# Planning a fixed issue order by a rehearsal with measured spacings: an attention and SwiGLU kernel on one core

## The chip, the cores and the metric

The kernel runs on one core of a Trainium2 chip. The metric is the device time of one execution in microseconds (us), as the median of several runs. The core has five engines that matter here, each with its own stream of instructions: TensorE (PE in the profile; its weight loads have a row of their own, PEld), VectorE (DVE), ScalarE (ACT), GpSimd (POOL) and SyncE (SP), which issues most transfers. [...]The program fixes the order of instructions on each engine.

## The reference

An attention over 32 inducing points is followed by a feed-forward block:

```python
# x (4, 12416, 128), inducing (32, 128)
def mab(q, kv):                       # softmax attention, scale 1/sqrt(C)
    s = scale * (q @ kv.transpose(0, 2, 1))
    a = np.exp(s - s.max(-1, keepdims=True))
    a /= a.sum(-1, keepdims=True) + 1e-09
    return a @ kv
h = mab(inducing, x)                  # 32 rows per batch
y = mab(x, h)                         # 12416 rows per batch
# then, with 49664 rows y, d_model 128, d_ff 1536:
yn   = y / sqrt(mean(y * y) + 1e-6) * rms_g
g    = yn @ w_gate                    # 128 -> 1536
val  = yn @ w_val                     # 128 -> 1536
out  = (g * sigmoid(g) * val) @ w_out # 1536 -> 128
```

## The kernel before

The rows of y are never made. Since y is a weighted sum of the 32 rows of h, the kernel multiplies h into the gate and value weights once a batch (`sg`, `sv`). What flows through the feed-forward block is the weights of the second attention, `a`.

**Units and slots.** Each of 4 batches has 25 units of up to 512 rows. d_ff is cut into 12 blocks of 128. One unit and one block make a *slot*: a gate matmul, a silu, a value matmul, a multiplication, and later a product with the block of `w_out`, which adds up over the 12 blocks in the PSUM tile `acc`. There are 1200 slots: 960 of 512 columns, 192 of 480 and 48 of 256.

```python
def slot(j, products, steps, tanh):
    g = bank()                                            # one of 5 PSUM banks
    nc.tensor.matmul(g[:, 0:T], sg[:, ts(j, P)], a[:, 0:T], start=True, stop=True)      # L681
    sl = silp.tile([P, 512], F32, name="silu")
    ...                                                   # (a variant with tanh, cut)
        nc.scalar.activation(sl[:, 0:T], g[:, 0:T], AF.Silu)                            # L689
    products()                                            # up to two products of earlier slots
    v = bank()
    nc.tensor.matmul(v[:, 0:T], sv[:, ts(j, P)], a[:, 0:T], start=True, stop=True)      # L692
    t = v if kinds.get((b, u, j)) == "sums" else up.tile([P, 512], F32, name="u")
    ...
        nc.vector.tensor_tensor(out=t[:, 0:T], in0=sl[:, 0:T], in1=v[:, 0:T], op=ALU.mult)   # L698
    steps()                                               # attention work, later parts of earlier slots
    if (b, u, j) in ready:
        soon(1, lambda: three(j, t))
    else:
        plain.append(lambda: project(wo[:, j, :], t[:, 0:T]))
```

**Kinds of blocks.** The product with `w_out` needs full fp32. A *plain* block does it as one fp32 product, which the trace shows as L616 x2. A *split* block takes the multiplied values apart into `hi`, `lo` and their difference `d`, and does three one-pass products in their place (L636, L638 and L616 with `more`). The first two add up in the single PSUM bank `u3` (shown as `u` on L636 and L638), the third in `acc`. The parts are made in two ways: "sums" on ScalarE, VectorE and one POOL operation, with the values left in their PSUM bank; "differences" with two operations on ScalarE and two on POOL.

```python
def three(j, t):
    while kws.get("out", 0) == RING:                      # RING = 4 places for hi, lo, d
        kara.pop(0)[1]()
    ...
    if kind == "sums":
        nc.scalar.activation(hi, v, AF.Copy, scale=(1.0 - 2.0 ** -13) * 2.0 ** -12)     # L663
        nc.vector.scalar_tensor_tensor(out=lo, in0=hi.bitcast(F32), scalar=-4096.0, in1=v, ...)   # L664
    else:
        up_ = third.tile([P, 512], F32R, name="hs")[:, 0:T]         # pool of one buffer
        nc.scalar.activation(up_, v, AF.Copy, scale=1.0 - 2.0 ** -13)                   # L668
        nc.gpsimd.tensor_tensor(out=lo, in0=v, in1=up_.bitcast(F32), op=ALU.subtract)   # L669
    def rest():
        if kind != "sums":
            nc.scalar.activation(hi, up_.bitcast(F32), AF.Copy, scale=2.0 ** -12)       # L673
        nc.gpsimd.tensor_tensor(out=d, in0=hi.bitcast(F32), in1=lo.bitcast(F32), op=ALU.subtract)  # L674
        kara.append((ready[b, u, j], lambda: project3(j, hi, lo, d)))
    soon(1, rest)
```

`soon(1, ...)` puts a step one slot later. When a unit's last split product is in, L641 (ScalarE) copies `u3` out.

**Which blocks are split, and when products are issued.** This is settled when the program is made. `loads` holds an estimate of each engine's work in each slot; a block is split, by sums if that fits and by differences if not, where the backlog of the next eight slots stays within LIMIT. `ready` is an estimated slot from which the product may be issued. In each slot `products()` then takes one or two of the waiting products, between the gate and the value matmul:

```python
loads = [[1.3, .68, .6, 0.0] ...]                         # us a slot: TensorE, VectorE, ScalarE, POOL
LIMIT = (0, 1.2, 1.2, 3.8)
RING, RESERVE = 4, 3
def products():
    now = b * NU * NJ + k
    count = max(len(plain) - 1, 0) + sum(at <= now for at, _ in kara)
    ...                                                   # exceptions near the exponentials, cut
    spare = ... else RESERVE
    for _ in range(min(count, 2 if count > spare else 1)):
        if kara and kara[0][0] <= now:
            kara.pop(0)[1]()
        else:
            plain.pop(0)()
```

**The seam.** Once for each of the attention sets (28 in all), the steps turn_a, square, turn_z, scale, apply, turn_b and split prepare the `a` of the next units. `scale` ends with the reciprocal root on POOL (L519, `rs`), which waits for a VectorE result of the same step (`ms`, L517). `apply` uses it on POOL too (L523). Before the change both stand in one slot.

**The next batch** runs its first attention and its weights beside the slots of the batch before; the fourth batch has none beside it.

Of the kernel before, what the change touches and what calls it, by code (L numbers as in the profile page):

```python
# [18 lines left out]
P = 128  # L19
R = 4  # L20
# [4 lines left out]
def kernel(  # L25
# [75 lines left out]
    RING, RESERVE = 4, 3  # L101
# [14 lines left out]
    third = pool("third", 1)  # L116
    silp = pool("silp", 3)
    up = pool("up", LAG + 3)
# [370 lines left out]
    def seam(b, s):  # L489
# [24 lines left out]
        def scale():  # L514
            ms = numbers("ms")
            nc.vector.reduce_sum(out=ms, in_=st["z"][rows, :, :], axis=AX.X)
            nc.vector.tensor_scalar(out=ms, in0=ms, scalar1=1.0 / C, scalar2=1e-6, op0=ALU.mult, op1=ALU.max)  # L517
            rs = st["rs"] = numbers("rs")
            nc.gpsimd.tensor_tensor(out=rs, in0=ms, in1=mhalf[rows, 0:n], op=ALU.pow)  # L519
# [18 lines left out]
        return [turn_a, square, turn_z, scale, apply, turn_b, split]  # L538
# [26 lines left out]
    def soon(k, step):  # L565

        waiting.append([k, step])
# [35 lines left out]
    def ffn(b, u):  # L603
# [6 lines left out]
        nk = sum((b, u, j) in ready for j in range(NJ))  # L610
# [43 lines left out]
        def three(j, t):  # L654

            while kws.get("out", 0) == RING:
                kara.pop(0)[1]()
            kws["out"] = kws.get("out", 0) + 1
            n = kws["n"] = (kws.get("n", 0) + 1) % RING
            hi, lo, d = (kws[name][:, n, 0:T] for name in ("hi", "lo", "d"))  # L660
            v, kind = t[:, 0:T], kinds[b, u, j]
            if kind == "sums":
                nc.scalar.activation(hi, v, AF.Copy, scale=(1.0 - 2.0 ** -13) * 2.0 ** -12)  # L663
                nc.vector.scalar_tensor_tensor(out=lo, in0=hi.bitcast(F32), scalar=-4096.0, in1=v,  # L664
                                               op0=ALU.mult, op1=ALU.add)
            else:
                up_ = third.tile([P, 512], F32R, name="hs")[:, 0:T]
                nc.scalar.activation(up_, v, AF.Copy, scale=1.0 - 2.0 ** -13)  # L668
                nc.gpsimd.tensor_tensor(out=lo, in0=v, in1=up_.bitcast(F32), op=ALU.subtract)  # L669

            def rest():
                if kind != "sums":
                    nc.scalar.activation(hi, up_.bitcast(F32), AF.Copy, scale=2.0 ** -12)  # L673
                nc.gpsimd.tensor_tensor(out=d, in0=hi.bitcast(F32), in1=lo.bitcast(F32), op=ALU.subtract)  # L674
                kara.append((ready[b, u, j], lambda: project3(j, hi, lo, d)))

            soon(1, rest)

        def slot(j, products, steps, tanh):
            g = bank()  # L680
# [9 lines left out]
            products()  # L690
# [9 lines left out]
            if (b, u, j) in ready:  # L700
                soon(1, lambda: three(j, t))
            else:
                plain.append(lambda: project(wo[:, j, :], t[:, 0:T]))
# [76 lines left out]
    turn_a, square, turn_z, scale, apply, turn_b, split = seam(0, 0)  # L780
# [6 lines left out]
    scale()  # L787
    weight[0, 1]["sign"]()
# [13 lines left out]
    if B > 1:  # L802
        for _ in range(R):
            load_channels(*pieces[1].pop(0))

    COST = {"turn_x": (0, .65), "scores1": (1.1, .7), "max2": (0, .85), "exp1_of": (0, 0, 1.3), "turn_e": (0, .69),
            "sum_h": (1.5, .29), "divide": (0, .8), "turn_h": (0, .8), "square_h": (0, .75), "stack": (1.1, 1.38),
            "scores2": (1.1, .69), "row_max": (0, .65), "sub_max": (0, 0, 0, 1.05), "exp2": (0, 0, 1.1), "table": (0, 0, 1.3),
            "turn_a": (0, .68), "square": (.9,), "turn_z": (0, 1.35), "scale": (0, .85, 0, 2.8), "apply": (0, 0, 0, 1.05),
            "turn_b": (0, .68), "split": (0, 0, .6, 1.26), "power": (0, .6), "power_number": (0, 0, .75), "upper": (0, .6),  # L810
            "upper_number": (0, 0, .65), "sign": (0, .7), "lower": (0, .7, 0, 1.3), "stack_of": (.9, 0, .6),
            "stack_low": (0, .7), "split_wo": (0, 0, .8, 1.6), "finish": ((0, .7, .6), (0, .7)),
            "sums": ((-.16,), (0, .7, .62), (0, 0, 0, 1.27)), "differences": ((-.16,), (0, 0, .63, 1.27), (0, 0, .63, 1.27))}
    loads = [[1.3, .68, .6, 0.0] for k in range(B * NU * NJ + 16)]

    def load(k, name, sign=1):
        cost = COST.get(name, ())
        for i, one in enumerate(cost if cost and isinstance(cost[0], tuple) else (cost,)):
            for e, us in enumerate(one):
                loads[k + i][e] += sign * us  # L820

    def schedule(b):
# [4 lines left out]
        def add(k, step, *args):  # L827
            plan.setdefault(int(k), []).append(lambda: step(*args))
            load(b * NU * NJ + int(k), step.__name__)

        def exponentials(k, step, first):
# [6 lines left out]
            for at in (k, k + len(groups)):  # L838
                load(b * NU * NJ + at, "table")
# [53 lines left out]
    for k, (b, s) in enumerate(order):  # L893
# [5 lines left out]
        for late_by, one in enumerate(following):  # L899
            for i, step in enumerate(seam(*one)):  # L900
                j = ((14, 17, 18, 21, 21, 29, 31) if k else (32, 33, 34, 35, 35, 39, 41))[i]
                n, j = divmod(j, NJ)
                at = (b, firsts[s] + n + late_by, j)
                seams.setdefault(at, []).append(step)
                load((b * NU + at[1]) * NJ + j, step.__name__)
# [7 lines left out]
    LIMIT = (0, 1.2, 1.2, 3.8)  # L913
    kinds, ready = {}, {}
    behind, out_at = [0.0] * 4, []

    def fits(k, kind):

        def ahead():
            now = list(behind)  # L920
            for i in range(k, k + 8):
                now = [max(0.0, x + one - loads[i][0]) for x, one in zip(now, loads[i])]
                yield list(now)

        before = list(ahead())
        load(k, kind)
        if all(x <= max(most, y + 0.1) for now, old in zip(ahead(), before) for x, y, most in zip(now, old, LIMIT)):
            return True
        load(k, kind, -1)

    for b, u in flat:
        load((b * NU + u + 1) * NJ + 4, "finish")
    for b, u in flat:
        marks = plans[b][1]
        for j in range(NJ):
            n = u * NJ + j
            k = b * NU * NJ + n
            out_at = [at for at in out_at if at >= k]
            if not (j >= NK or b == 0 and (u < 2 or n < 26) or (b, u) == flat[-1] and j > 6 or len(out_at) >= RING or
                    any(n - 1 <= e <= n + 3 for e in marks)):  # L940
                for kind in ("sums", "differences"):
                    if fits(k, kind):
                        kinds[b, u, j] = kind
                        left, last, at = behind[3], k + 2, k
                        for at in range(k, last):
                            left = max(0.0, left + loads[at][3] - loads[at][0])
                        late = 1.4 + left + loads[last][3] + max(behind[1:3])
                        at = last
                        while late > 0.1:
                            late -= loads[at][0]  # L950
                            at += 1
                        ready[b, u, j] = at
                        out_at.append(ready[b, u, j] - 1)
                        break
            for e in range(1, 4):
                behind[e] = max(0.0, behind[e] + loads[k][e] - loads[k][0])

    for b in range(B):
        plan, marks = plans[b]

        order = [(u, j) for u in range(NU) for j in range(NJ)]
        if not b:
            order[:2 * NJ] = sorted(order[:2 * NJ], key=lambda one: (one[1] // R, one))
        unit = {}
        for k, (u, j) in enumerate(order):

            def steps():
# [7 lines left out]
                for step in plan.get(k, ()):  # L975
                    step()
                for step in seams.get((b, u, j), ()):
                    step()
# [3 lines left out]
            def products():  # L982


                now = b * NU * NJ + k
                count = max(len(plain) - 1, 0) + sum(at <= now for at, _ in kara)
                hold = any(k < e <= k + 2 for e in marks)
                if hold and count < LAG:
                    return
                spare = 1 if any(e <= k < e + 4 for e in marks) or (b, u) == flat[-1] else RESERVE  # L990
                for _ in range(min(count, 2 if count > spare else 1)):
                    if kara and kara[0][0] <= now:
                        kara.pop(0)[1]()
                    else:
                        plain.pop(0)()
# [4 lines left out]
    while kara or plain:  # L1000
        (plain.pop(0) if plain else kara.pop(0)[1])()
# [32 lines left out]
```

## Time and profile before

| | before |
|---|---|
| time, median of 3 runs | 1706.56 us (1705.57 to 1708.16) |
| span of the profiled run | 1706.2 us |
| mean granted TensorE clock | 0.995 |
| VectorE, ScalarE, POOL busy | 80%, 71%, 69% |
| split blocks | 612 of 1200: 415 by sums, 197 by differences |
| `hs` of ScalarE (L668), idle before | 88.8 us, of which 68.5 waiting for POOL L669 |
| root on POOL (L519), 28 times | 2709 ns mean, 134.5 us idle before |

How to read it: "busy" is the time in which an engine has at least one instruction running. A line such as `PE acc L616 <- POOL xn L674` names who waited, writing what, and for whose instruction; behind the colon are the total in us, how often, and the longest. Names such as `xn` can stand for other things than the code's: the ring of hi, lo and d lies in the buffers `xn`. A timeline line has the start, the duration, the engine, the line and operation, and in brackets the idle time before it with its releaser. A count x2 means that two instructions in a row were merged. Ends of matmuls are modelled and overlap the next start.

### The profile page before, as it was taken

Reading aid. Unit: us, or ns where it says so; the run is one execution under the profiler, and the core shown is the slowest. Engines: PE = TensorE matmul, PEld = TensorE weight load, DVE = VectorE, ACT = ScalarE, POOL = GpSimd, SP = SyncE. Lnnn points to the kernel's source line nnn. Section 1 sums busy time; section 2 is a strip of 40 time slices with the busy share of each in tenths; the row PEclk is TensorE's granted clock in tenths of the full one; section 3 lists DMA queues with packets and bytes.
Section 4 is the critical chain, followed back from the end, with each engine's and each line's share of the span. In section 5 each row is a group of like instructions: output and inputs, shape, how many; then the busy total and the mean of one; then the engine's idle time right before and its main releaser. Section 6 shows DMA issues by size and latency. Waiting matters only on the chain. (4 is left out here: it accounts for less than half of the span.)

```text
span 1706.2 us, 24769 instructions
## 1 busy us (share of the span) xinstructions
PE 1649.8 (97%) x6992; PEld 1063.0 (62%) x6992; DVE 1371.8 (80%) x2350; ACT 1214.5 (71%) x2247; POOL 1173.4 (69%) x944
## 2 busy tenths in 40 slices
PE   8989999999999999999999999999999999999998
PEld 6546666656575665665667666556566666666666
DVE  5878887788788887778878888778878888888887
ACT  4557777667686676666768676667677787787776
POOL 1347784768486674577758675477757888888886
PEclk9999999999999999999999999999999999999999
DMA  6345524343443141524335324153211212112211
GB/s 249 87 68 82 103 46 97 73 97 58 70 77 67 31 88 29 128 66 81 67 53 82 55 40 84 31 122 84 54 30 30 38 32 38 34 29 38 37 32 28
DMA packets 389177, 112.47 MB, mean 66 GB/s; under 512 B 365073, under 2 KB 369713, under 8 KB 386481
## 3 DMA queue, kind: packets, MB, share of 16 engines
q1 hardware_dynamic: 388304, 110.82, 32.9%
q8 instruction: 55, 0.90, 0.2%
q14 instruction: 82, 0.66, 0.1%
q10 hardware_dynamic: 736, 0.08, 0.0%
HBM read 53.95 MB, written 27.00 MB: 47 GB/s over the span
## 5 line engine op out<-in xcount | busy, mean ns | idle before, releaser
L674 POOL TENSOR_TENSOR xn<-xn,xn 128x512 fp32r<-128x512 f32 (+2 forms) x612 | 758.1, 1253 | 247.1 <-DVE xn L664 133.5
L689 ACT ACTIVATE silu<-gv 128x512 f32<-128x512 f32 (+2 forms) x1186 | 687.4, 584 | 309.1 <-PE gv L681 296.0
L692 PE MATMUL gv<-a,sv 128*128 128x512 f32 (+2 forms) x1188 | 676.7, 570 | 4.8 <-ACT silu L689 3.8
L698 DVE TENSOR_TENSOR u<-silu,gv 128x512 f32<-128x512 f32 (+2 forms) x771 | 510.0, 665 | 190.1 <-PE gv L692 126.3
L616 PE MATMUL acc<-u,wo 128*128 128x512 f32 (+1 forms) x1176 | 587.7, 584 | 4.5 <-DVE u L698 4.3
L681 PE MATMUL gv<-a,sg 128*128 128x512 f32 (+2 forms) x1188 | 487.1, 410 | 4.3 <-ACT silu L689 2.6
L681 PEld LDWEIGHTS gv<-a,sg 128*128 128x128 f32 x1188 | 224.4, 189 | 209.4 <-ACT silu L689 54.5
L698 DVE TENSOR_TENSOR gv<-silu,gv 128x512 f32<-128x512 f32 (+2 forms) x415 | 277.7, 672 | 94.0 <-PE gv L692 61.6
L692 PEld LDWEIGHTS gv<-a,sv 128*128 128x128 f32 x1188 | 225.0, 189 | 169.4 <-issue 81.0
L664 DVE SCALAR_TENSOR_TENSOR xn<-xn,gv 128x512 fp32r<-128x512 f32 (+2 forms) x415 | 273.0, 658 | 7.3 <-ACT xn L663 3.9
L663 ACT ACTIVATE xn<-gv 128x512 fp32r<-128x512 f32 (+2 forms) x415 | 242.5, 584 | 47.0 <-DVE gv L698 40.9
L669 POOL TENSOR_TENSOR xn<-u,hs 128x512 fp32r<-128x512 f32 (+2 forms) x197 | 249.2, 1265 | 28.5 <-ACT hs L668 18.1
L616 PE MATMUL acc<-xn,more 128*128 128x512 f32 (+2 forms) x612 | 245.7, 401 | 23.0 <-POOL xn L674 22.8
L616 PEld LDWEIGHTS acc<-u,wo 128*128 128x128 f32 x1176 | 220.2, 189 | 60.4 <-issue 8.8
L636 PE MATMUL u<-xn,xn 128*128 128x512 f32 (+2 forms) x612 | 237.9, 389 | 4.2 <-ACT o L641 3.8
L668 ACT ACTIVATE hs<-u 128x512 fp32r<-128x512 f32 (+2 forms) x197 | 122.7, 623 | 88.8 <-POOL xn L669 68.5
L519 POOL TENSOR_TENSOR rs<-ms,mhalf 128x16 f32<-128x16 f32 (+2 forms) x28 | 75.9, 2709 | 134.5 <-DVE ms L517 122.8
L616 PEld LDWEIGHTS acc<-xn,more 128*128 128x128 f32 x612 | 115.1, 188 | 71.6 <-POOL xn L674 50.7
L636 PEld LDWEIGHTS u<-xn,xn 128*128 128x128 f32 x612 | 115.2, 188 | 33.3 <-ACT o L641 10.2
L638 PE MATMUL u<-xn,xn 128*128 128x512 f32 (+2 forms) x321 | 124.3, 387 | 0.0
L673 ACT ACTIVATE xn<-hs 128x512 fp32r<-128x512 f32 (+2 forms) x197 | 121.2, 615 | 0.0
L638 PE MATMUL u<-xn,more 128*128 128x512 f32 (+2 forms) x291 | 113.2, 389 | 0.0
(150 smaller groups left out, 1062.3 us busy)
## 6 DMA issues: line engine op xcount, KB each, us to landing
out_dram<-o SPq DMA_DIRECT2D x320, 64.0 KB, 2.0
xT<-in_x_dram SPq DMA_DIRECT2D x60, 256.0 KB, 4.7
xn<-in_x_dram SPq DMA_DIRECT2D x60, 256.0 KB, 4.9
a<-hi SPq DMA_DIRECT2D x156, 64.0 KB, 2.0
a<-lo SPq DMA_DIRECT2D x156, 64.0 KB, 2.0
xn<-in_x_dram SPq DMA_DIRECT2D x5, 1024.0 KB, 10.0
xn<-w SPq DMA_DIRECT2D x18, 256.0 KB, 3.0
out_dram<-o SPq DMA_DIRECT2D x64, 60.0 KB, 2.0
```

The lines of the kernel that those rows point to most:

```text
L616: nc.tensor.matmul(acc[:, 0:T], lhsT, rhs, start=st["left"] == NJ, stop=st["left"] == 1)
L636: nc.tensor.matmul(ups[:, 0:T], weight_of(0, j), hi, start=st["k"] == nk, stop=False)
L638: nc.tensor.matmul(ups[:, 0:T], weight_of(1, j), lo, start=False, stop=not st["k"])
L663: nc.scalar.activation(hi, v, AF.Copy, scale=(1.0 - 2.0 ** -13) * 2.0 ** -12)
L664: nc.vector.scalar_tensor_tensor(out=lo, in0=hi.bitcast(F32), scalar=-4096.0, in1=v, op0=ALU.mult, op1=ALU.add)
L668: nc.scalar.activation(up_, v, AF.Copy, scale=1.0 - 2.0 ** -13)
L669: nc.gpsimd.tensor_tensor(out=lo, in0=v, in1=up_.bitcast(F32), op=ALU.subtract)
L674: nc.gpsimd.tensor_tensor(out=d, in0=hi.bitcast(F32), in1=lo.bitcast(F32), op=ALU.subtract)
L681: nc.tensor.matmul(g[:, 0:T], sg[:, ts(j, P)], a[:, 0:T], start=True, stop=True)
L689: nc.scalar.activation(sl[:, 0:T], g[:, 0:T], AF.Silu)
L692: nc.tensor.matmul(v[:, 0:T], sv[:, ts(j, P)], a[:, 0:T], start=True, stop=True)
L698: nc.vector.tensor_tensor(out=t[:, 0:T], in0=sl[:, 0:T], in1=v[:, 0:T], op=ALU.mult)
```

## The change

All costs are replaced by spacings read from traces, and the planning by a rehearsal: while the program is made, a small model walks through all slots with a clock for each engine, decides the kind of each block by the backlog it sees, and notes for each slot which products go ahead of the gate matmul and which ahead of the value matmul. The program then follows these notes. Besides, the number of blocks held outstanding goes from three to six, with one more `u` buffer; the root becomes a step of its own; and the single buffer `hs` goes, its place taken by the block's own `d`.

```diff
-    RING, RESERVE = 4, 3
+    RING, RESERVE = 4, 6
-    third = pool("third", 1)
-    up = pool("up", LAG + 3)
+    up = pool("up", LAG + 4)
...
+            st["ms"] = ms
+
+        def root():
             rs = st["rs"] = numbers("rs")
-            nc.gpsimd.tensor_tensor(out=rs, in0=ms, in1=mhalf[rows, 0:n], op=ALU.pow)
+            nc.gpsimd.tensor_tensor(out=rs, in0=st["ms"], in1=mhalf[rows, 0:n], op=ALU.pow)
...
-            while kws.get("out", 0) == RING:
-                kara.pop(0)[1]()
+            assert kws.get("out", 0) < RING
...
-                up_ = third.tile([P, 512], F32R, name="hs")[:, 0:T]
-                nc.scalar.activation(up_, v, AF.Copy, scale=1.0 - 2.0 ** -13)
-                nc.gpsimd.tensor_tensor(out=lo, in0=v, in1=up_.bitcast(F32), op=ALU.subtract)
+                nc.scalar.activation(d, v, AF.Copy, scale=1.0 - 2.0 ** -13)
+                nc.gpsimd.tensor_tensor(out=lo, in0=v, in1=d.bitcast(F32), op=ALU.subtract)
...
         def slot(j, products, steps, tanh):
+            products(0)
             g = bank()
...
-            products()
+            products(1)
             v = bank()
...
-    loads = [[1.3, .68, .6, 0.0] for k in range(B * NU * NJ + 16)]
+    TAIL = {"PE": .17, "DVE": .09, "ACT": .11, "POOL": .04}
+    MADE = {"sums": ((-.16,), (0, .6, .49), (0, 0, 0, 1.25)), "differences": ((-.16,), (0, 0, .53, 1.25), (0, 0, .52, 1.25))}
+    loads = [[1.29, .6, .5, 0.0] for k in range(B * NU * NJ + 24)]
...
-                j = ((14, 17, 18, 21, 21, 29, 31) if k else ...)[i]       # slots of the seam's steps
+                j = ((14, 17, 18, 21, 22, 23, 29, 31) if k else ...)[i]
...
-    LIMIT = (0, 1.2, 1.2, 3.8)
+    LIMIT = (0, 0.8, 0.8, 2.6)
+    def rehearse():
+        ...
+        def issue(kind, to):
+            ...
+            if kind == "plain":
+                end = run("PE", 0.858 * w, t)
+            else:
+                if st["three"] == 0:
+                    run("PE", 0, split["u3"])
+                end = run("PE", 0.697 * w, t)
+        ...
+        def choose(to, most):              # up to `most` products that are ready, split ones first
+        def fill(to, until):               # products ahead of a bank that comes free later than 0.25 us from now
+            while until > at["PE"] + 0.25:
+                now = at["PE"] + 0.05
+                kind = next((kind for kind in ("three", "plain") if has(kind, now)), None)
+                if kind is None:
+                    break
+                issue(kind, to)
+        ...
+        def slot(b, k, u, j, tanh):
+            kind = decide(b, k, u, j)      # by the backlog of the modelled clocks and LIMIT
+            first, second = picks[b, k] = [], []
+            gi = bank()
+            fill(first, free[gi])
+            g = run("PE", 0.2325 * w, free[gi])
+            silu = run("ACT", 0.5 * w, g)
+            ...
+            least = 1 if near(...) or (b, u) == flat[-1] else RESERVE + 2 * near(b, k, -2, 0)
+            choose(second, min(2, max(0, split["all"] - least + 1)))
+            ...
+            fill(second, free[vi])
+            v = run("PE", 0.2325 * w, free[vi])
+            t = run("DVE", 0.6 * w, v, silu)
...
-            def products():
-                ...                        # the rule by counts, shown above
+            def products(some):
+                for kind in picks[b, k][some]:
+                    (plain if kind == "plain" else kara).pop(0)()
```

## The prediction

> **What bounds the kernel now.** I read the busy shares first, then TensorE's timeline, then the waits, then the groups.
>
> ```profile
> PE 1649.8 (97%) x6992; PEld 1063.0 (62%) x6992; DVE 1371.8 (80%) x2350; ACT 1214.5 (71%) x2247; POOL 1173.4 (69%) x944
> ```
>
> TensorE is the bound: no other engine is above 80%. But 97% doesn't say how much a better order can give, because a matmul's record overlaps the next one. The Trainium skill ("Perfetto Trace Analysis", Identifying the Most-Contended Engine) says that the busy share of matmuls is no good measure of how near one is to the limit. The trace agrees: the records below last 0.40 us and begin 0.23 us apart. So I use the distance from start to start. This is TensorE's timeline in a quiet stretch (start, duration, instruction):
>
> ```profile
> 810.22 0.80 PE L692 MATMUL gv<-a,sv 128*128 128x512 f32 x1
> 810.85 0.40 PE L681 MATMUL gv<-a,sg 128*128 128x512 f32 x1
> 811.09 0.39 PE L636 MATMUL u<-xn,xn 128*128 128x512 f32 x1
> 811.32 0.40 PE L638 MATMUL u<-xn,xn 128*128 128x512 f32 x1
> 811.55 0.40 PE L616 MATMUL acc<-xn,more 128*128 128x512 f32 x1
> 811.79 0.39 PE L692 MATMUL gv<-a,sv 128*128 128x512 f32 x1
> 812.02 0.39 PE L681 MATMUL gv<-a,sg 128*128 128x512 f32 x1
> 812.25 1.02 PE L616 MATMUL acc<-u,wo 128*128 128x512 f32 x2
> 812.71 0.80 PE L692 MATMUL gv<-a,sv 128*128 128x512 f32 x1
> 813.34 0.40 PE L681 MATMUL gv<-a,sg 128*128 128x512 f32 x1
> ```
>
> A one-pass matmul (gate L681, value L692, each of a split product's three) takes 0.2325 us of TensorE. A plain product (L616 x2) with the value matmul after it takes 813.34 - 812.25 = 1.09, so 0.858 alone. A split product is 3 x 0.2325 = 0.697. **Each block moved from plain to split saves 0.16 us of the bound engine.** Counting L636 and L681: 612 of 1200 blocks are split now, 352 of 716 (49%) from 300 to 1300 us and 200 of 320 (63%) after 1300, where no attention of a next batch runs beside.
>
> With these spacings I added up the timeline between successive gate matmuls. In 983 of 1199 intervals there are only gate, value and products: they last 1243.4 us against 1160.6 undisturbed, so **82.8 us are lost**. The first recorded wait in the interval is on POOL in intervals worth 27.2, on the silu in 13.6, on VectorE in 5.4; 36.6 are in intervals with no recorded matmul wait. The other 216 intervals hold attention matmuls and can't be sized this way; at the same rate, 0.084 each, they hold some 18 us. In all about **100 us, 6% of the time, are order and not work**. The waits name its parts:
>
> ```profile
> PE acc L616 <- POOL xn L674: 22.8, 22, 2.0
> PEld gv L681 <- ACT silu L689: 55.7, 183, 0.8
> PEld gv L692 <- ACT silu L689: 28.1, 52, 1.4
> PEld gv L681 <- DVE u L698: 25.7, 78, 0.8
> ACT hs L668 <- POOL xn L669: 68.5, 62, 3.7
> POOL rs L519 <- DVE ms L517: 122.8, 27, 13.4
> ```
>
> Columns: total, times, longest. The first is a split product whose third operand d isn't made. The next three are weight loads for a gate or value matmul whose PSUM bank is still being read; the load normally hides behind the matmul before, and only what sticks out delays TensorE, which is where I put the 36.6 with no recorded matmul wait. The last two are on engines that aren't the bound.
>
> What the last has to do with the first is seen once per attention set (from 1353 to 1603 us such waits come 62.5 us apart):
>
> ```profile
> 1350.06 2.90 POOL L519 TENSOR_TENSOR rs<-ms,mhalf 128x16 f32<-128x16 f32 x1 [2.17 <-DVE ms L517]
> 1353.04 1.05 POOL L523 TENSOR_TENSOR sc<-sc,rs 128x512 f32<-128x512 f32 x1
> 1354.04 4.99 POOL L674 TENSOR_TENSOR xn<-xn,xn 128x512 fp32r<-128x512 f32 x4
> 1355.36 0.50 PE L616 MATMUL acc<-xn,more 128*128 128x512 f32 x1 [1.40 <-POOL xn L674]
> ```
>
> POOL stands 2.17 us at the root's wait, works 2.90 on it and 1.05 on its use; four d queue behind; TensorE has begun the split product two matmuls earlier and stops for 1.40.
>
> **What the Trainium skill says.** "TensorE: Matmul & The Clock Gate", Architectural detail: TensorE can pull weight loads ahead, but ScalarE, VectorE and GpSimd are strict FIFO. The trace agrees: the four d above had to wait for the root although they don't use it. "GPSIMD Engine Reference", 3.1 Elementwise: a two-input elementwise operation takes GpSimd about 2.6 cycles an element, VectorE about 1. Here 1253 ns for 128x512 on POOL (L674) against 665 on VectorE (L698): a difference block, with two POOL operations, is the dear kind, and POOL's time is worth guarding. "Perfetto Trace Analysis", Optimization Strategy: a gap that repeats regularly can mean too few buffers. For `hs` this fits, 62 waits of 1.1 us.
>
> **The change part by part.**
>
> 1. *Rehearsal and places.* A product is put where its operand should be ready, and a product is put ahead of a gate or value matmul whose bank isn't free. Waits on d, 27.2 us: mostly late by one to two us at the root, which the rehearsal knows (2.9 for root, 1.25 for d). I leave 6: **-21**. Bank waits, 13.6 + 5.4 + 36.6 = 55.6: products ahead can fill them, but each is only about a tenth to a quarter of a us, at the edge of what spacings rounded to 0.05 can place (the rule fills only above 0.25). I take a little over a third: **-20**. Attention intervals, 18: a third, **-6**.
>
> 2. *Root in its own slot.* It removes no work. The root is issued one slot (about 1.3 us) later and its use another one later, so POOL may do d's between. Of the 122.8 us that POOL waits, 27 x 1.3 = 35 could go; none is TensorE's. Its gain is inside the 21.
>
> 3. *No single buffer.* `hs` becomes the block's own `d`. ScalarE loses up to 68.5 us of standing, but it idles 29% anyway; the benefit is that a silu isn't stuck behind, so inside the 20. One more `u` buffer takes the space.
>
> 4. *Six outstanding instead of three.* No instruction is added; there is more to choose from, and a product is more often old enough. It is what makes 1 possible. TensorE has one more constraint: a split product before a plain one may start the next group early, and the single bank u waits for the copy out (L641, 10.2 us of weight-load waits now).
>
> 5. *Kinds.* The planned price of VectorE falls from 0.68 to 0.60 a slot, and from 0.70 to 0.60 a "sums" block. The trace supports 0.60: two L698 in a row end after 1.29 us with 0.68 each, so they are 0.61 apart. The old plan thought VectorE fuller than it is. A slot frees 0.08; another sums block needs 0.60 plus the 0.16 by which its slot gets shorter, so 0.08/0.76 = 0.105 blocks more a slot, over some 1170 slots about 120. Against this stand tighter limits of backlog (1.2 to 0.8, POOL 3.8 to 2.6), four ring places and two blocks of twelve that are never split. I take two thirds, **+80 blocks, about 690**: 80 x 0.161 = **-13**. They cost VectorE 80 x 0.66 = 53 us and POOL 80 x 1.25 = 100, beside TensorE: VectorE comes to 1425 of 1650, 86%, POOL to 77%.
>
> 6. New waits from fuller VectorE and POOL: **+6**, a choice.
>
> Sum: -21 - 20 - 6 - 13 + 6 = -54, so 1706.6 - 54 = **1652 us**.
>
> **Rivals.**
> *VectorE takes over.* Sums blocks hold their bank until the second VectorE operation; with 86% busy a burst of attention work makes banks late and gives back what 1 saved. For it: the 78 waits on L698. Against: VectorE idles 334 us now, mostly waiting for TensorE (L698 on L692, 126.3). Then 1675 to 1700.
> *The rehearsal is wrong by a little, everywhere.* The order is fixed in the program, and matmuls don't pass each other; a product placed 0.05 us after its modelled readiness waits if d is late by 0.3. Then POOL waits spread out instead of vanishing: 1685 to 1715. Against: spacings near those in the trace, and a modelled TensorE that is a bit too fast makes operands earlier, not later.
> *The mix shrinks.* If the tighter limits win, say 60 fewer split blocks, +10, waits still gone: about 1675.
> *Everything works.* Two thirds of the 100 us and 120 blocks: 1706 - 67 - 19 = 1620.
>
> **Range and chances.** The last rival sets the low end, 1620; the other end is half of the wait gain lost and no gain from kinds, 1706 - 24 + 6 = 1688. Two percent is 1672.4; my sum is 20 below it, and only the first three rivals cross it. A slower kernel needs a rehearsal that misplaces products generally. Faster by over 2%: 0.75; within: 0.22; slower: 0.03.
>
> **What would show it.** Split products (L636 count) near 690, the surplus among sums. TensorE's wait on L674 under 8 us. The ScalarE wait on POOL L669 gone, POOL's wait at the root under 90. The weight-load waits on silu and L698 down by a third. Lost time by the same addition around 50 instead of 83. VectorE at 85 to 87%. The prediction is wrong if split blocks are fewer than 612, if waits on L674 or L641 at TensorE grow, or if bank waits grow with VectorE.

## The result and the profile after

The changed kernel takes 1645.53 us (1644.39 to 1646.33) against 1706.07 beside it: a ratio of 0.9643, with a 95% interval of 0.9626 to 0.966. The predicted time was 1652. The busy shares after, from the page:

```profile
PE 1620.6 (99%) x6983; PEld 1070.2 (65%) x6983; DVE 1431.0 (87%) x2469; ACT 1156.8 (70%) x2104; POOL 1007.2 (61%) x804
```

VectorE is busier, as foreseen; but POOL, foreseen at 77%, went down to 61%. The groups of the page say why (L665 is before's L664, the others keep their numbers):

```profile
L674 POOL TENSOR_TENSOR xn<-xn,xn 128x512 fp32r<-128x512 f32 (+2 forms) x603 | 750.1, 1255 | 451.1 <-DVE xn L665 271.4
...
L665 DVE SCALAR_TENSOR_TENSOR xn<-xn,gv 128x512 fp32r<-128x512 f32 (+2 forms) x537 | 354.4, 660 | 9.8 <-ACT xn L664 5.5
...
L669 POOL TENSOR_TENSOR xn<-u,xn 128x512 fp32r<-128x512 f32 (+1 forms) x66 | 85.1, 1289 | 19.3 <-ACT xn L668 19.1
```

Every split block makes one d, so there are 603, nine *fewer* than before. 537 are made by sums (415 before) and only 66 by differences (197 before). The plan has moved work from POOL to VectorE and has not split more.

The waits after, answering to those of before (L618 is the product, L682 gate, L693 value, L699 the multiplication, L521 the root):

```profile
POOL rs L521 <- DVE ms L516: 68.0, 21, 14.4
...
PEld gv L682 <- ACT silu L690: 45.8, 180, 1.0
...
PEld gv L682 <- DVE u L699: 23.9, 84, 0.8
...
PEld gv L693 <- ACT silu L690: 5.9, 20, 0.7
...
PE acc L618 <- POOL xn L674: 2.6, 4, 0.7
```

TensorE's wait on d fell from 22.8 to 2.6; for silus the weight loads of the value matmul wait 5.9 instead of 28.1, those of the gate matmul 45.8 instead of 55.7. ScalarE's wait on L669 is gone from the list.

**Where the 62 us went.** The addition of the prediction, made on both timelines with every record counted, gives three parts. (The 1160.6 and 82.8 in the prediction should have been 1169.0 and 74.3: its sum missed 8.4 us of plain products. So the 36.6 without a recorded matmul wait are 28, and the 100 us of order are some 92. Of the 216 intervals that it sets aside, about half hold attention matmuls; the others follow one that does.)

| | before | after |
|---|---|---|
| gates, values and products at undisturbed spacings | 1442.9 | 1444.2 |
| lost in intervals with nothing else | 74.3 | 17.8 |
| attention matmuls and what is lost around them (in their interval and the next) | 126.9 | 120.3 |

The work grew by 1.3, the two others fell by 63.1. So the gain is not less work. Nearly all of it is time that TensorE stood, but not quite all. In the profiled run before, TensorE's granted clock is half (0.50) in three stretches, 13.7 us together; this is one of them (the first line is a row of a table by stretches: its length, the busy time of each engine, and third from the end the clock):

```profile
656.40:659.80 3.40, 3.40 (x8) 1.91 (x7) 1.76 (x3) 2.77 (x5) 3.40 (x4) 0.50 0.00 0
...
655.33 0.50 PE L616 MATMUL acc<-xn,more 128*128 128x512 f32 x1 [1.99 <-POOL xn L674]
...
656.80 0.63 PE L616 MATMUL acc<-xn,more 128*128 128x512 f32 x1
657.23 0.63 PE L692 MATMUL gv<-a,sv 128*128 128x512 f32 x1
```

One-pass matmuls begin 0.43 us apart here, not 0.23. The seven intervals that these stretches touch last 9.4 us longer than undisturbed. One wait of 3.1 is in that; most of the other 6 is in intervals without a recorded matmul wait, which the prediction put down to weight loads. In the changed kernel one such stretch of 3.4 us is left while TensorE works. So some 4 of the 63 us are clock, an estimate from these spacings. What brings a stretch on is not shown. Each of the three begins 2.2 to 3.1 us after TensorE came to a stand, of 2.0 to 3.1 us; but in two runs below, with the root's slot alone and without `hs`, stands of 3.15 and 1.99 us bring none.

Which part of the change removed the standing is another question, and the profile alone would have misled me on it.

### The profile page after: what moved, and what is told of

Its sections match the earlier page's. It is cut to its first block, busy times and chain, and to the rows that moved or that the text cites. A ratio compares the mean times of both kernels' runs of the same rounds, so it can differ in the third digit from the quotient of the medians.

```text
span 1644.2 us, 24663 instructions
## 1 busy us (share of the span) xinstructions
PE 1620.6 (99%) x6983; PEld 1070.2 (65%) x6983; DVE 1431.0 (87%) x2469; ACT 1156.8 (70%) x2104; POOL 1007.2 (61%) x804
## 4 chain that ended last, share of the span: by engine, by line
PE 89%; DVE 2%; ACT 2%; issue 1%; POOL 1%; SPq 1%; DMA 1%; DVEq 0%; POOLq 0%; ACTq 0%
PE acc L618 35%; PE gv L682 17%; PE gv L693 15%; PE u L640 8%; PE u L638 8%; PE gv L327 3%; PE gv L504 1%; PE gv L383 1%; ACT sc L444 1%; POOL rs L521 0%; DVE u L699 0%; SPq L147 0%; PE gv L458 0%; DVE xn L665 0%; ACT silu L690 0%
## 5 line engine op out<-in xcount | busy, mean ns | idle before, releaser
L693 PE MATMUL gv<-a,sv 128*128 128x512 f32 (+2 forms) x1188 | 680.2, 573 | 0.5 <-ACT silu L690 0.2
L618 PE MATMUL acc<-u,wo 128*128 128x512 f32 (+2 forms) x1194 | 591.6, 580 | 0.0
L682 PE MATMUL gv<-a,sg 128*128 128x512 f32 (+2 forms) x1188 | 486.2, 409 | 3.9 <-ACT silu L690 2.4
L699 DVE TENSOR_TENSOR u<-silu,gv 128x512 f32<-128x512 f32 (+2 forms) x650 | 423.3, 659 | 59.0 <-PE gv L693 41.7
L699 DVE TENSOR_TENSOR gv<-silu,gv 128x512 f32<-128x512 f32 (+2 forms) x536 | 359.8, 673 | 86.8 <-PE gv L693 66.7
L665 DVE SCALAR_TENSOR_TENSOR xn<-xn,gv 128x512 fp32r<-128x512 f32 (+2 forms) x537 | 354.4, 660 | 9.8 <-ACT xn L664 5.5
L682 PEld LDWEIGHTS gv<-a,sg 128*128 128x128 f32 x1188 | 224.5, 189 | 207.4 <-ACT silu L690 45.0
L664 ACT ACTIVATE xn<-gv 128x512 fp32r<-128x512 f32 (+2 forms) x537 | 314.6, 586 | 52.2 <-DVE gv L699 44.1
L693 PEld LDWEIGHTS gv<-a,sv 128*128 128x128 f32 x1188 | 224.4, 189 | 157.4 <-issue 77.1
L618 PEld LDWEIGHTS acc<-u,wo 128*128 128x128 f32 x1194 | 224.0, 189 | 55.3 <-issue 12.0
L618 PE MATMUL acc<-xn,more 128*128 128x512 f32 (+2 forms) x603 | 235.1, 390 | 2.6 <-POOL xn L674 2.6
L618 PEld LDWEIGHTS acc<-xn,more 128*128 128x128 f32 x603 | 113.3, 188 | 29.9 <-POOL xn L674 6.3
L638 PEld LDWEIGHTS u<-xn,xn 128*128 128x128 f32 x603 | 113.4, 188 | 24.1 <-issue 4.2
L521 POOL TENSOR_TENSOR rs<-ms,mhalf 128x16 f32<-128x16 f32 (+2 forms) x28 | 75.9, 2710 | 68.8 <-DVE ms L516 68.0
L669 POOL TENSOR_TENSOR xn<-u,xn 128x512 fp32r<-128x512 f32 (+1 forms) x66 | 85.1, 1289 | 19.3 <-ACT xn L668 19.1
L640 PE MATMUL u<-xn,more 128*128 128x512 f32 (+2 forms) x247 | 95.9, 388 | 0.0
L640 PEld LDWEIGHTS u<-xn,xn 128*128 128x128 f32 x356 | 66.9, 188 | 15.2 <-issue 0.2
L629 DVE STREAM_TRANSPOSE o<-o 128x512 f32<-128x512 f32 (+2 forms) x92 | 63.0, 685 | 0.0
```

The source lines that it names most:

```text
L521: nc.gpsimd.tensor_tensor(out=rs, in0=st["ms"], in1=mhalf[rows, 0:n], op=ALU.pow)
L618: nc.tensor.matmul(acc[:, 0:T], lhsT, rhs, start=st["left"] == NJ, stop=st["left"] == 1)
L638: nc.tensor.matmul(ups[:, 0:T], weight_of(0, j), hi, start=st["k"] == nk, stop=False)
L640: nc.tensor.matmul(ups[:, 0:T], weight_of(1, j), lo, start=False, stop=not st["k"])
L669: nc.gpsimd.tensor_tensor(out=lo, in0=v, in1=d.bitcast(F32), op=ALU.subtract)
```

## Experiments

Two theories stood at the start. *Placing*: the waits went because the rehearsal puts each product where its operand is ready. *Kinds*: they went because POOL has fewer difference blocks to make. As rivals to both there were the depth of six and the two small parts, root and `hs`. In the runs called "kinds held" the blocks to split come from a fixed table.

### Kinds and placing apart

The changed kernel with before's kinds:

```diff
-            kind = decide(b, k, u, j)
+            kind = table_of_before[b, u, j]
```

> The changed kernel, but which blocks are split, and how, is taken from the kernel before (415 by sums, 197 by differences) as a fixed table; the rehearsal only places the products. Placing theory (the waits went because products are issued when their operands are ready): 1645 to 1660 us, waits of TensorE on POOL's d under 8 us. Kinds theory (the waits went because 131 fewer difference blocks leave POOL with 166 us less work, so d is early): 1680 to 1700 us, waits on d near the 22.8 of before. Half each: about 1670.

Measured: 1658.69 us, ratio 0.972 (0.9706 to 0.9735), TensorE's wait on d 4.5 us. With POOL as full as before (1175.5 us) most of the gain is there. Kinds are not needed for it; they are worth the 13 us from here to the changed kernel. One thing comes with the table: where it asks for a split block while all four ring places are taken, the rehearsal first has to issue a product. Here 125 gates stand right behind a split product, most of them for this reason, and in the changed kernel none; the 13 us hold what that costs.

The reverse, the kernel before with the changed kernel's kinds:

```diff
-                    if fits(k, kind):
-                        kinds[b, u, j] = kind
+                        kinds[b, u, j] = table_of_after[b, u, j]
```

> The other half: the kernel before in all (its rule of placing by counts and estimated slots, hs, root inside scale, three outstanding), with the split blocks of the changed kernel (537 by sums, 66 by differences) as a fixed table. Placing theory: 1695 to 1715 us. Kinds theory: 1650 to 1665 us, POOL about 61% busy and few waits on d.

Measured: 1680.29, ratio 0.9848 (0.9831 to 0.9864), between both expectations. In this run TensorE's wait on d (0.7 us) and ScalarE's on `hs` (4.7) are nearly gone too. So one set of waits can be removed in two ways, and neither theory had said so. Up to here "placing" looked like the winner. But the first of these kernels holds the small parts too, and the next runs took them by themselves.

### The small parts alone

The root's own slot, in the kernel before, with its kinds held. The root is taken out of `scale` as a step `root`, and the steps get these slots:

```diff
-                j = ((14, 17, 18, 21, 21, 29, 31) if k else ...)[i]
+                j = ((14, 17, 18, 21, 22, 23, 29, 31) if k else ...)[i]
```

> The kernel before with one part of the change: the root a step of its own, one slot after scale, and its use one slot later again; the split blocks are held as before by a fixed table. Theory that the root's place by itself mends the waits on d (POOL no longer stands and then works 3.95 us in one go): 22.8 us of TensorE's waits on d fall to 8 or less, 1688 to 1694 us. Placing theory (the products have to be told of the root): the waits on d stay above 14 us, 1698 to 1706.

Measured: 1692.95, ratio 0.9915 (0.9898 to 0.9931). TensorE's waits in it (L619 is the product, L695 value, L684 gate):

```profile
PE gv L695 <- ACT silu L692: 7.1, 12, 1.3
PE acc L619 <- DVE u L701: 6.2, 6, 3.1
PE gv L684 <- ACT silu L692: 5.7, 17, 0.8
```

POOL's d has left the top of the list; it is 1.3 us in all. The placing did move a little: the old rule's estimate holds the root's load, which now stands one slot later, and products differ in 79 of 1200 slots. But for 18 of the 22 waits on d of before, 20.4 of the 22.8 us, the product that had waited stands in the same slot as before. So it is POOL's order that removed them, and not a placing that knows the root: POOL waits 22.7 us for `ms` at the root instead of 122.8, and at 23 of 28 roots it does one d between the root and its use.

No `hs`, in the kernel before:

```diff
-                nc.scalar.activation(up_, v, AF.Copy, scale=1.0 - 2.0 ** -13)
+                nc.scalar.activation(d, v, AF.Copy, scale=1.0 - 2.0 ** -13)
```

> The kernel before with one part of the change: no single buffer hs, its place taken by d. Same blocks, same order. The ScalarE waits on POOL (68.5 us) go in either case. If they hold up silus and with them TensorE: 1695 to 1701 us. If ScalarE has the time (idle 29%): 1703 to 1708, no change that matters.

Measured: **1681.86**, ratio 0.9856 (0.9838 to 0.9874), some 25 us from one buffer; TensorE's instructions are the same in the same order. Both expectations failed: the gain is well above the 5 to 11 us of the first, and the second saw none. TensorE's waits, first before and then without `hs` (L615 is the product, L679 the gate):

```profile
PE acc L616 <- DVE u L698: 4.3, 3, 3.1
PE gv L692 <- ACT silu L689: 4.0, 9, 0.6
...
PE acc L615 <- POOL xn L672: 20.9, 23, 2.0
...
PE gv L679 <- ACT silu L687: 2.0, 10, 0.2
```

This is the other half: the waits on d stay, those on silus and multiplied values go (of the latter 1.2 us are left, and the weight loads of the value matmul wait 10.2 us for silus instead of 28.1). How `hs` did it can be read in the timeline of before, all engines, near one root:

```profile
305.85 2.90 POOL L519 TENSOR_TENSOR rs<-ms,mhalf 128x16 f32<-128x16 f32 x1 [3.11 <-DVE ms L517]
...
312.30 1.28 POOL L669 TENSOR_TENSOR xn<-u,hs 128x512 fp32r<-128x512 f32 x1
...
313.62 0.63 ACT L668 ACTIVATE hs<-u 128x512 fp32r<-128x512 f32 x1 [3.73 <-POOL xn L669]
...
314.15 0.58 ACT L689 ACTIVATE silu<-gv 128x512 f32<-128x512 f32 x1
...
314.76 0.69 DVE L698 TENSOR_TENSOR u<-silu,gv 128x512 f32<-128x512 f32 x1 [4.60 <-ACT silu L689]
...
314.79 0.49 PE L692 MATMUL gv<-a,sv 128*128 128x512 f32 x1 [0.56 <-ACT silu L689]
```

POOL is late after the root, so it reads `hs` late. ScalarE's next writing of `hs` stands 3.73 us, and the silu behind it, which has nothing to do with it, stands too; VectorE then waits 4.60 for that silu, and the value matmul is held for 0.56 by its bank. A buffer that two engines which aren't the bound hand to each other has stopped the bound.

A part of both gains goes with the clock. The runs of before show a mean granted clock of 0.995 to 0.998, those without `hs` 0.997 to 1.0. Where all show 0.997, the times are 1705.3 and 1705.5 us before, 1685.5 without `hs` and 1693.0 with the root's slot: 20 and 12 us in place of 25 and 15, each from one or two runs.

Both parts:

> The kernel before with two parts of the change: the root's own slot and no hs; same split blocks, old rule of placing, three outstanding. One part alone gave 1693, the other 1682. If they remove different waits they add up: 1664 to 1670 us. If both come off the same waits: 1678 to 1684. Against the run with old kinds and rehearsed placing (1658.7) this shows what the rehearsed placing with six outstanding adds by itself: 5 to 11 us in the first case, 20 or more in the second.

Measured: 1664.61, ratio 0.9752 (0.9736 to 0.9768): they add up. About two thirds of the whole gain (42 of 61 us) come from these two, without any rehearsal.

### What is left for the plan

All of the change but the rehearsed placing and the depth, that is the two parts and the new kinds under the old rule:

> The same with the split blocks of the changed kernel (537 by sums, 66 by differences): all of the change but the rehearsed placing and the six outstanding. New kinds alone gave 1680, with waits on silus and multiplied values left and hardly any on d or hs, so the two parts have little to remove any more: 1672 to 1680 us. If the placing was of no account: within 6 us of 1645.

Measured: 1680.53, ratio 0.9845 (0.9831 to 0.986), the same as with the new kinds alone (1680.29). The new kinds make the kernel with both parts *slower* by 16 us. Its waits at TensorE (L618 product, L693 value, L682 gate):

```profile
PE gv L693 <- ACT silu L690: 10.3, 24, 0.7
PE acc L618 <- DVE u L699: 7.8, 14, 1.0
PE gv L682 <- ACT silu L690: 4.2, 13, 0.5
```

In its timeline 435 gate matmuls are followed at once by a value matmul, without a product between; in the kernel with both parts and the old kinds 64, in the changed kernel 38. Instead, 366 gates follow a split product directly. The old rule issues a product at such a place only when the ring of four is full: the new kinds come too densely for its estimated slots, and products are forced out where they don't help. So the new kinds need the rehearsed placing, with which they gain 13.

The changed kernel with three outstanding, own kinds held:

```diff
-    RING, RESERVE = 4, 6
+    RING, RESERVE = 4, 3
```

> The changed kernel with its own kinds as a fixed table, but three blocks outstanding in the rehearsal instead of six. A split block needs about three slots until d is made, so with three outstanding TensorE should often find nothing ready. Depth theory (the rehearsal's own clock grows by 144 us): 1750 to 1800 us, with long waits on d and on the multiplied values. Placing theory without need of depth (a right order at any depth): within 15 us of 1645.

Measured: 1783.37, ratio 1.0451 (1.0435 to 1.0466). The size was right, by the rehearsal's own clock, but not the waits I named:

```profile
PE gv L682 <- ACT silu L690: 28.3, 45, 1.2
PE gv L693 <- ACT silu L690: 26.0, 83, 1.2
```

They are on banks that a silu still reads. Nothing is ready in many slots, so 371 gates are followed at once by the value matmul. TensorE hardly waits for d (0.4 us), since the plan doesn't issue it early; it runs out of filling between gate and value.

Six outstanding under the old rule, without `hs` (its space is needed for the ninth `u`); the edit in short:

```diff
-                for _ in range(min(count, 2 if count > spare else 1)):
+                for _ in range(max(0, min(count, 2, outstanding - least))):   # least: 5
```

> The kernel before with six blocks held outstanding by its old rule of counts and estimated slots (no hs, whose space the ninth u buffer takes; same blocks). Depth theory (with enough blocks in hand any rule finds one that is ready): 1660 to 1675 us. Placing theory (depth helps against waits on silu and multiplied values, but the estimated slots still call for d too early at the root): 1690 to 1700, waits on d still near 20 us.

Measured: 1681.53, the same as without `hs` alone (1681.86), waits on d 21.3 us. Depth by itself is worth nothing to the old rule, which had enough in hand: "three" and "six" don't count the same things in the two rules (the old one leaves out blocks whose d isn't made). Counted in the traces, the blocks still without their product at the end of a slot are 5.2 on average before, 5.9 in this run, 6.0 in the changed kernel and 3.8 with three in the rehearsal. So the change made the kernel hardly deeper, and the run with three is shallower than the kernel before.

### Does the rehearsal need to know of the root?

```diff
-            "root": (0, 0, 0, 2.9), ...
+            "root": (0, 0, 0, 0), ...
```

> The changed kernel with its own split blocks as a fixed table, but the rehearsal isn't told that the root takes POOL 2.9 us (it counts 0). All instructions are the same in number; only products near the root are placed as if d were there earlier. If the gain at the root comes from placing by measured spacings: 28 roots with up to two us each return, TensorE's wait on d 15 to 35 us, 1660 to 1680 us. If it comes from depth, fewer difference blocks or the root's own slot: within 4 us of 1645.

Measured: 1645.82. With the kinds held, not one product moved: the order of all instructions is that of the changed kernel, so the time is that of a repeat. What it says is that the placing, for these kinds, doesn't depend on the root's price; TensorE's wait on d stays 2.6 us.

Root and use back in the slot of scale, in the changed kernel:

> The changed kernel with its own kinds as a fixed table, but root and its use back in the slot of scale; the rehearsal knows it. If a rehearsal that knows of the late d places around it: within 3 us of 1645. If the root's slot is needed also here: 1652 to 1662 us with waits on d of 10 us and more.

Measured: 1645.92, and products differ in 8 slots. The root's slot is worth 14 us in the kernel before and nothing here. Around one root after the change (POOL and the products of TensorE):

```profile
1355.45 2.90 POOL L521 TENSOR_TENSOR rs<-ms,mhalf 128x16 f32<-128x16 f32 x1 [1.25 <-DVE ms L516]
...
1358.32 1.28 POOL L674 TENSOR_TENSOR xn<-xn,xn 128x512 fp32r<-128x512 f32 x1
1359.56 1.05 POOL L525 TENSOR_TENSOR sc<-sc,rs 128x512 f32<-128x512 f32 x1
1359.65 0.19 PEld L618 LDWEIGHTS acc<-xn,more 128*128 128x128 f32 x1 [1.14 <-POOL xn L674]
1359.65 0.50 PE L618 MATMUL acc<-xn,more 128*128 128x512 f32 x1 [0.71 <-POOL xn L674]
```

One d stands behind the root, where there were four; a weight load waits 1.14 for it, and its matmul 0.71. There are four such waits of a product left in the whole run.

### Is there more on either side?

```diff
-    LIMIT = (0, 0.8, 0.8, 2.6)
+    LIMIT = (0, 1.2, 1.2, 3.8)
```

> The changed kernel with the limits of backlog of the kernel before (1.2, 1.2, 3.8 in place of 0.8, 0.8, 2.6): 641 split blocks (592 by sums, 49 by differences) instead of 603. If each further split block still saves 0.16 us of TensorE, as step 5 of the prediction has it: 38 x 0.16 = 6 us less, about 1639. If VectorE, at 87%, has become the second bound (rival: VectorE takes over), waits on PSUM banks and multiplied values eat it: 1645 or more.

Measured: 1651.53, ratio 0.9676 (0.9662 to 0.9691).

```profile
PE 1622.5 (98%) x7021; PEld 1070.8 (65%) x7021; DVE 1464.7 (89%) x2530; ACT 1159.4 (70%) x2131; POOL 1030.3 (63%) x825
```

By the addition, the work fell by 5.8 us as expected, and the lost time grew from 17.8 to 25.1, that around attention from 120.3 to 122.2. So the 38 further blocks cost more than they save. That it is VectorE, at 89%, is likely but not separated: the limits of ScalarE and POOL were loosened with its own.

Seven outstanding:

> The changed kernel with seven outstanding instead of six; the rehearsal then splits 608 blocks instead of 603, and its own clock falls by 2.4 us. Depth theory: 1641 to 1645 us. If six is enough and further depth only holds buffers longer: 1645 to 1650.

Measured: 1646.07, ratio 0.9644 (0.9629 to 0.9658): six is enough. None of these versions beats the changed kernel.

## Why the prediction was right, and where not

The time, 1645.5, lies in the range and 6 below the predicted value. That it came so near is partly luck. The waits were to give 41 (47 less the 6 for new ones) and fewer blocks' work 13; in fact the work gave nothing and the waits 63, so two errors cancelled. By the prediction's own sign, fewer than 612 split blocks, its account of the kinds is wrong.

**The bound and what could be had: right.** About 100 us (92 by the corrected sum) were called order and not work; the time lost fell by 63.1, some 4 of it clock, and the work did not fall.

**Part 5, kinds, failed.** "+80 blocks, about 690: -13" is the term; it measured nine blocks fewer and +1.3 us. I read the lower prices and took the tighter limits for a third of the effect. The run with looser limits shows that they are not too tight: its 38 further splits lose 6 us. That the surplus lies with sums came true, at the expense of differences instead of on top of them.

**Part 3, no single buffer, was mis-sized.** I gave it a share of the 20 for bank waits because "it idles 29% anyway". Alone it measured 25 us (20 at equal clock). The prediction quotes the Trainium skill ("TensorE: Matmul & The Clock Gate", Architectural detail) that ScalarE, too, works strictly in order, and applies it to POOL only; the trace agrees for ScalarE, where a silu stood behind the 3.73 us wait for `hs`. It also quotes "Perfetto Trace Analysis", Optimization Strategy, on repeated gaps without that page's condition, that they lie on the engine that should be saturated. The gaps of `hs` lie on ScalarE, so the page alone does not say that they cost anything; the run does.

**Part 2, the root, was undersized as a cause.** "35 could go; none is TensorE's" is the step that failed: with the slot alone 100 us of POOL's wait went, TensorE's wait on d fell from 22.8 to 1.3, and 14 to 15 us were gained (12 at equal clock). The reason given for the 21, that the rehearsal knows the root, failed too: with the root priced at nothing not one product moves. In the finished kernel the slot isn't needed any more. POOL has 166 us less to do there and the products are placed differently; which of the two makes the slot needless is not shown.

**Part 1, the rehearsal, was oversized as placing and had an effect I gave it no room for.** Placing with six outstanding, on top of both small parts, measured 6 us (1664.61 to 1658.69), against 47 in my sum of all wait terms, in which the small parts were contained. The 6 are for kinds it did not choose. Its larger service is to choose kinds that go with its placing: 13 us.

**Part 4, six in place of three, was misread.** "It is what makes 1 possible" took the two numbers for the same count. The kernel before already had 5.2 blocks in hand, the changed one has 6.0, and six under the old rule gained nothing.

In a sequence: no `hs` -25 (by its ratio), then by the measured times root -17, placing with depth -6, kinds -13. The order matters, as the new kinds under the old rule show.

**Part 6, +6 for new waits,** cannot be seen apart. VectorE came to 87% (predicted 86), by another way.

**Signs named ahead.** Right: TensorE's wait on d under 8 (2.6), ScalarE's on L669 gone, POOL's at the root under 90 (68.0), VectorE. Wrong: the split count. Mixed: the weight loads' waits on silus fell by 38%, from 83.8 to 51.7, nearly all at the value matmul; those of the gate on the multiplication L698 (L699 after), which writes `u` or the bank, rose from 42.1 to 54.2 with VectorE fuller. Lost time by the addition is 17.8, far below the 50 I named. Weight-load waits are a poor measure of it: these alone are 106 us after, so most stay hidden behind a matmul.

Left open: whether the kinds' 13 us come from POOL's relief, from *where* the split blocks stand, or from the products that the old table forces out. All changed with one table, and no run here holds one of them.

## What to carry to other kernels

Before planning a better order, look for a buffer of one between two engines that aren't the bound, and for one long operation with its use in the same place of a queue; here these two small repairs gave 42 of 61 us. An idle share doesn't excuse a wait on an engine that works strictly in order, as ScalarE did here: ask what stands behind it. And a plan and its placing are one thing; a set of choices that gains 13 us under one rule of placing loses 16 under another.

## What the runs showed that I had not expected

The model of a few spacings, made while the program is built, foretold a bad plan's cost well: its clock rose by 144 us for three outstanding, and the chip took 138 more. For small differences it was less use: it saw 0.2 us of gain where looser limits lost 6, and 2.4 of gain where seven outstanding gave none.
